# Sums of a seven-product output matmul moved from GpSimd to VectorE, with a planner that counts their shared port

## The chip, the cores and the metric

One Trainium2 chip, one of its cores. The time is device microseconds of one execution, the median of several. Engines: TensorE (PE) multiplies, VectorE (DVE), ScalarE (ACT) and GpSimd (POOL) work element by element, SyncE (SP) issues the DMAs, which start in the order of its queue.

## The reference

```python
# attention: batch 4, 12 heads, 448 tokens, 64 per head
scores = scale * np.matmul(q, k.transpose(0, 1, 3, 2))
scores = np.einsum('bhij,hg->bgij', scores, w_pre)
attn = exp(scores - max) / (sum + 1e-09)
attn = np.einsum('bhij,hg->bgij', attn, w_post)
x = np.matmul(attn, v)            # as [1792 tokens, 768]
# two products behind it
h = x @ w_in                      # [1792, 2048]
g = h * np.clip(h + 3.0, 0.0, 6.0) / 6.0
return g @ w_out                  # [1792, 768]
```

w_in and w_out are float64 and reach the kernel as 64-bit integers.

## The kernel before

The attention runs in 180 steps over rows of scores; a step has TensorE mix the heads, VectorE take the maximum (line 474), ScalarE the exponential (475), GpSimd the scaling and the low half of a two-part fp16 number (483, 486), and TensorE mix again (502). `av` (line 518) multiplies with v and leaves x, as a high and a low fp16 half (544, 545), in groups G0 to G7 (two for a batch). `moe1` (688) makes h and g of a group, 16 column blocks `fc` each, in three fp16 products (704), and stores g to DRAM (`gd`).

The last product, g @ w_out, is done with seven block products for a batch instead of eight: P1, P2 (stage 1) and P6, P7, P4, P5, P3 (stage 2). P1 and P2 take blocks of g and w_out as they are; the other five take sums and differences of blocks. Each operand is split into a high half (ScalarE, line 847) and a low half (VectorE, `scalar_tensor_tensor`, line 848), `ws_P` and `wg` or `gx_P` for short in the trace, and `product` (980) runs 24 matmuls for each of 3 row blocks m. `add` (1004) brings the PSUM sums together on VectorE.

w_out is decoded while the attention still runs: `w_out_decode` (678) is called every 4th step from step 72 on, with low urgency (priority 2000 and more), for 24 pieces of 128x512. It reads the integers, ScalarE and VectorE turn them into fp32 (585 to 600), and a store puts them into DRAM (`wod`, 683). After the attention, `w_one` loads 12 pieces for P1 and P2, and `w_two` loads all 24 again; `w_two_put` has GpSimd make four sums for each of six sets (`minus`, line 861) before the five splits. `g_two` (953) loads four blocks of g for each half of a batch and has GpSimd make four sums of 128x896 in the same way.

The order of all instructions on every engine is fixed when the kernel is built. A list planner (`Plan.run`, line 153) takes each operation's engine, a written duration, its inputs and outputs and a priority (lower goes first), and simulates: an engine that is free takes the ready operation of lowest priority. VectorE and GpSimd are independent of each other in it. The loads of the last product wait for `close_a` (line 802): all that the attention's buffers are used for must be done. The tiles of P6 and P7's w_out lie in a pool that opens when the last group of `moe1` no longer needs the first half of w_in (`close_w0`, 834), those of P4, P5 and P3 when `moe1` is through altogether (`close_w`, 830). The two buffers `slots` (863) hold the operands of P1 and P2; they follow the attention's `A` buffers in one ring of two.

Of the kernel before, what the change touches and what calls it, by code (L numbers as in the profile page):

```python
# [25 lines left out]
P = 128  # L26
# [18 lines left out]
G2_AT, G2_BY = 1080, 100  # L45
LATE_W = 'P4', 'P5', 'P3'
# [7 lines left out]
class Op:  # L54
    __slots__ = ("eng", "dur", "fn", "prio", "n", "succ", "order", "ready", "end", "bytes", "no", "mode", "takes", "then")
# [49 lines left out]
class Plan:  # L105
# [7 lines left out]
    STAY = 8.0  # L113

# [3 lines left out]
    def op(self, eng, dur, fn, r=(), w=(), prio=0.0, after=(), nbytes=0, mode=0):  # L118
        o = Op()
        o.eng, o.dur, o.fn, o.prio, o.bytes, o.mode = eng, dur, fn, prio, nbytes, mode  # L120
        o.succ, o.order, o.n, o.ready, o.no, o.end, o.takes, o.then = [], [], 0, 0.0, len(self.ops), None, [], None
        deps = {}

        def need(d):
            deps[d.no] = d

        for x in r:
            b, key = x if isinstance(x, tuple) else (x, None)
            for k, u, wr in b.uses:
                if wr and (k is None or key is None or k == key):  # L130
                    need(u)
        for x in w:
            b, key = x if isinstance(x, tuple) else (x, None)
            if b.pool and not b.uses and b not in o.takes:
                o.takes.append(b)
            if b not in self.bufs:
                self.bufs[b] = []
            self.bufs[b].append(o)
            for k, u, wr in b.uses:
                if k is None or key is None or k == key:  # L140
                    need(u)
        for u in after:
            need(u)
        for x, wr in [(x, False) for x in r] + [(x, True) for x in w]:
            b, key = x if isinstance(x, tuple) else (x, None)
            b.uses.append((key, o, wr))
        for d in deps.values():
            d.succ.append(o)
            o.n += 1
        self.ops.append(o)  # L150
        return o

    def run(self):
# [10 lines left out]
        bw, mode, then = 0.0, None, None  # L164

# [27 lines left out]
        while True:  # L193
# [34 lines left out]
            o.end = t + o.dur  # L228
            if e == "PE" and self.filler:
# [22 lines left out]
def body(ctx: ExitStack, tc: tile.TileContext, q4, kT, vj, wpre0, wpost0, ident0, w_in, w_out, outT):  # L252
# [32 lines left out]
    def dve(dur, fn, r, w, prio):  # L285
        return plan.op("DVE", dur, fn, r, w, prio)
# [295 lines left out]
    def decode(raw, o, n, st, prio, cost):  # L582
# [21 lines left out]
        return lambda: [dve(cost[2 + i], f, [raw] * (i > 0), [o], prio + 0.3 + 0.1 * i) for i, f in enumerate((b1, b2, b3))]  # L604

    def pow64(top, am1, t, p, r):
# [4 lines left out]
        DVE.tensor_scalar(r(), r(), 2.0 ** 14, None, op0=ALU.mult)  # L611

# [3 lines left out]
    def w_in_item(fc, after=()):  # L616
# [6 lines left out]
        o = buf(rot, [P, DM], F32, "wf", f"wf_i{fc}", 3)  # L623
        st, am1, t, r = (buf(rot, [P, 1], F32, f"wi_{x}", f"wi{x}_{fc}", 4) for x in ("st", "am", "t", "r"))
        dma(786432, lambda: SP.dma_start(raw(), w_in[fc]), [], [raw], at, after)
        rest = decode(raw, o, DM, (st, st), at, (0.81, 0.94, 0.5, 1.15, 1.25))
# [15 lines left out]
        if fc % 4 == 0:  # L642
            act(0.82, lambda: ACT.activation(h(), o(), AF.Copy, scale=r()), [o, r], [(w, (0, fc))], at + 2)
            dve(1.0, lambda: DVE.scalar_tensor_tensor(l(), o(), r(), h(), op0=ALU.mult, op1=ALU.subtract), [o, r, (w, (0, fc))], [(w, (1, fc))], at + 2)
# [25 lines left out]
    def w_out_read(k, raw, o, at, after):  # L670
        plan.op("SP", 0.5, lambda: SP.dma_start(raw()[:, :4 * P], w_out[k // 4, k % 4]), [], [raw], at, after, 524288)
        decode(raw, o, 4 * P, ((wo_st, k), lambda: wo_st()[:, k:k + 1]), at, (0.57, 0.66, 0.35, 0.64, 0.64))()
        if k == 11:
            w_out_scale(0, 12, 1, at + 2)
        if k == 23:
            w_out_scale(1, 24, 4, at + 2)

    def w_out_decode(k, at, after):
        d = wo_dram[k] = Buf(lambda: dram.tile([P, 4 * P], F32, name=f"wod_{k}"))
        raw = buf(rot, [P, NCC * P], I64, "stw", f"wo_{k}", 2)  # L680
        o = buf(rot, [P, DM], F32, "wf", f"wf_d{k}", 3)
        w_out_read(k, raw, o, at, after)
        dma(262144, lambda: SP.dma_start(d(), o()[:, :4 * P]), [o], [d], at + 5)
# [116 lines left out]
    for b, gi, at in scales:  # L800
        g_scale(b, gi, at + 8)
    close_a = plan.op("X", 0.0, ph_a.close, prio=0, after=[o for o in plan.ops])
# [12 lines left out]
    for z in (wpre0_f, wpost0_f, wpre8, wpost_n, wpost_h, wpost_l, T_all, *(z for k, g in rings.items() if k[0] == "T" for z in g.all)):  # L815
# [27 lines left out]
    def load(nbytes, fn, r, w, at, after):  # L843
        plan.op("SP", 0.5, fn, r, w, at, after, nbytes)

    def split(src, r, to, key, n, at, after, big):
        plan.op("ACT", 0.95 if big else 0.63, lambda: ACT.activation(to(0), src(), AF.Copy, scale=r()), [src.b, r], [key], at, after)
        dve(1.3 if big else 0.9, lambda: DVE.scalar_tensor_tensor(to(1), src(), r(), to(0), op0=ALU.mult, op1=ALU.subtract), [src.b, r], [key], at + 0.1)  # L848

    class View:  # L850
        def __init__(self, b, fn):
            self.b, self.fn = b, fn

        def __call__(self):
            return self.fn()

    def whole(b):
        return View(b, lambda: b())
# [4 lines left out]
    slots = [buf(apool, [P, 11520], F16, "A", f"wg_{i}", 2) for i in range(2)]  # L863

    def w_view(t, z, i):
        return t()[:, :6144].rearrange("p (z m f c) -> p z m f c", z=2, m=3, f=8)[:, z, i // 2, 4 * (i % 2):4 * (i % 2) + 4]

    def g_view(t, at, z):
        return t()[:, at:at + 1792].rearrange("p (z f n) -> p z f n", z=2, f=4)[:, z]

    WS = {}

    def w_item(i):
        m, q = divmod(i, 2)
        return 4 * m + q, 4 * m + q + 2, 12 + 4 * m + q, 14 + 4 * m + q

    def w_tile(name):
        return gbuf([P, 4 * P], F32, "wr", name, WR)

    def w_load(k, at, name):  # L880
        if k < WO_EARLY:
            t = w_tile(name)
            load(262144, lambda: SP.dma_start(t(), wo_dram[k]()), [wo_dram[k]], [t], at, [close_a])
        else:
            raw = gbuf([P, 4 * P], I64, "stw", f"{name}_raw", 2)
            t = w_tile(name)
            w_out_read(k, raw, t, at, [close_a])
        return t

    def w_put(name, t, i, at, z, after):  # L890
        src = View(t, lambda: t().rearrange("p (f c) -> p f c", f=4))
        b = WS[name]
        split(src, later_r(z), lambda y: w_view(b, y, i), (b, (name, i)), 4 * P, at, after, False)

    class LaterR:
        pass

    def later_r(z):
        return wo_r[z]

    def w_one(i, at):
        for name, k in zip(("P1", "P2"), w_item(i)[:2]):
            t = w_load(k, at, f"w{name}_{i}")
            w_put(name, t, i, at, 0, [close_a])

    def w_two(i, at):
        k11, k12, k21, k22 = w_item(i)
        a21, a22 = w_load(k21, at, f"w21_{i}"), w_load(k22, at + 1, f"w22_{i}")
        a11, a12 = w_load(k11, at + 2, f"w11_{i}"), w_load(k12, at + 3, f"w12_{i}")
        s1 = w_tile(f"ws1_{i}")  # L910
        todo2.append((i, at, a11, a12, a21, a22, s1))

    def w_two_put(i, at, a11, a12, a21, a22, s1):
        minus(s1, a21, a22, ALU.add, at, False, [close_a])
        minus(a21, a11, a21, ALU.subtract, at + 1, False)
        minus(a11, s1, a11, ALU.subtract, at + 2, False)
        minus(a12, a12, a11, ALU.subtract, at + 3, False)
        for j, (name, t) in enumerate((("P6", a11), ("P7", a21), ("P4", a22), ("P5", s1), ("P3", a12))):
            w_put(name, t, i, at + 4 + j, 1, [close_a, close_w if name in LATE_W else close_w0])

    GP, later_home = {}, []
# [4 lines left out]
    def g_load(b, kk, half, i, at):  # L926
        t = g_tile(f"g{kk}{half}_{b}_{i}_{at}")
        f = 8 * kk + 4 * i
        keys_ = [(g_dram[b], (k, gi)) for k in (f // 2, f // 2 + 1) for gi in range(1 + half)]
        load(458752, lambda: SP.dma_start(t(), g_dram[b]()[:, f:f + 4, half * NH:half * NH + NH]), keys_, [t], at, [close_a])  # L930
        return t

    def g_put(name, b, i, t, at, home):
# [8 lines left out]
        GP[name, b, i] = (lambda z: g_view(x, o, z)), (x, (name, b, i))  # L942
        split(whole(t), g_s[b], lambda z: g_view(x, o, z), (x, (name, b, i)), 4 * NH, at, after, True)

    def g_one(b, at):
        for kk, name in ((0, "P1"), (1, "P2")):
            for i in range(2):
                n = 4 * b + 2 * kk + i
                t = g_load(b, kk, 0, i, at + 10 * kk + i)
                home = (slots[n // 3], 6144 + 1792 * (n % 3)) if n < 6 else None  # L950
                g_put(name, b, i, t, at + 10 * kk + i + 2, home)
# [52 lines left out]
    def add(out, ps, u, us, key_o, key_u, after):  # L1004
        plan.op("DVE", 0.37, lambda: DVE.scalar_tensor_tensor(out(), ps()[:, :NH], us(), u(), op0=ALU.mult, op1=ALU.add), [ps, us, key_u], [key_o], -80, [after])

    def stage1(b, at):
        us = scale(0, b)
        ua = uas[b] = [lambda m=m: ua_all()[:, b, m * NH:(m + 1) * NH] for m in range(3)]
        for m in range(3):  # L1010
            ps = product("P1", b, m, at)
            act(0.35, lambda m=m, ps=ps: ACT.activation(ua[m](), ps()[:, :NH], AF.Copy, scale=us()), [ps, us], [(ua_all, (b, m))], -80)
# [25 lines left out]
    WS["P1"], WS["P2"] = slots  # L1038
    for b in range(B):
        g_one(b, -300 + 60 * b)  # L1040
        if b == 0:
            for i in range(6):
                w_one(i, -290 + i)
# [45 lines left out]
```

## Time and profile before

| | us |
|---|---|
| median of 3 runs | 847.67 |
| lowest, highest | 846.43, 854.39 |
| profiled execution | 839.76 |
| its span, first to last instruction | 837.9 |

The profile is of one execution. Its page gives the busy time of each engine and the chain of work that ended last; other views give a table of stretches, instructions in order of time, waits, and groups by line. A group of instructions is named as line, engine, operation, output <- inputs, and partitions x elements; `x24` is a count. The PE clock is the share of full speed that was granted.

### The profile page before, as it was taken

The numbers are of one execution on the slowest core, as the hardware profiler recorded it, in microseconds if no ns is written. First come the engines' busy times: TensorE is split into PE (matmuls) and PEld (weight loads), VectorE is DVE, ScalarE is ACT, GpSimd is POOL, SyncE is SP. The second block draws the span as 40 slices with busy tenths as digits, with TensorE's granted clock in tenths as the row PEclk, the third lists the DMA queues.
The fourth block names the chain that finished last, engine by engine and source line by source line (L and its number), as shares of the span: only waits on it lengthen the run. The fifth ranks groups of instructions, "written<-read, shape, count | busy, mean of one in ns | idle before, by whom it ended". The sixth has DMA issues, their size and how long they took to land.

```text
span 837.9 us, 27650 instructions
## 1 busy us (share of the span) xinstructions
PE 793.0 (95%) x11588; PEld 639.2 (76%) x11588; DVE 594.0 (71%) x1129; ACT 529.5 (63%) x1043; POOL 483.5 (58%) x590
## 2 busy tenths in 40 slices
PE   8997899999999999999999989999999957999998
PEld 2554567577777767677777767889999956999998
DVE  4588887788657656967775876753865999878432
ACT  2477879887986766868886778865844735233200
POOL 2245789878775635667574567764027588495300
PEclk9799999999999999999999999999999988999999
DMA  7979977886588678878879787632993651655101
GB/s 258 309 233 307 319 224 230 277 258 213 165 286 255 206 215 277 276 241 258 272 232 291 226 275 253 194 100 63 362 336 113 189 171 41 197 156 160 56 18 51
DMA packets 107649, 179.32 MB, mean 214 GB/s; under 512 B 8308, under 2 KB 80084, under 8 KB 107524
## 3 DMA queue, kind: packets, MB, share of 16 engines
q1 hardware_dynamic: 107524, 177.55, 67.8%
q8 instruction: 91, 1.49, 0.7%
q14 instruction: 34, 0.28, 0.1%
HBM read 112.33 MB, written 65.18 MB: 212 GB/s over the span
## 4 chain that ended last, share of the span: by engine, by line
PE 63%; DVE 11%; DMA 10%; POOL 6%; issue 4%; ACT 4%; SPq 1%; ACTq 0%; DVEq 0%; POOLq 0%
PE single L704 19%; PE single L988 18%; PE single L502 8%; PE single L467 6%; PE pair L376 6%; PE single L539 5%; DVE ws_P L848 3%; DMA wo<-in_w_out 3%; POOL el L486 2%; POOL e L483 2%; DMA wi<-in_w_in 2%; DVE nb L474 2%; DVE gx_P L848 1%; DMA v<-in_vj 1%; PE single L743 1%
## 5 line engine op out<-in xcount | busy, mean ns | idle before, releaser
L704 PE MATMUL single<-x,wi 128*128 128x208 f16 (+1 forms) x2304 | 228.9, 260 | 4.4 <-ACT e L475 2.9
L704 PEld LDWEIGHTS <-wi 128*128 128x128 f16 x2304 | 214.4, 98 | 23.5 <-issue 16.9
L486 POOL TENSOR_TENSOR el<-e,eh 128x448 f16<-128x448 f32 x156 | 168.3, 1098 | 48.2 <-ACT eh L485 46.3
L988 PEld LDWEIGHTS <-ws_P 128*128 128x128 f16 x1440 | 141.5, 100 | 17.4 <-DVE ws_P L848 7.7
L483 POOL TENSOR_SCALAR e<-e,r 128x448 f32<-128x448 f32 x180 | 128.2, 723 | 43.3 <-DVE r L478 39.0
L475 ACT ACTIVATE e<-single,nb 128x448 f32<-128x448 f32 x180 | 113.3, 637 | 33.6 <-DVE nb L474 32.8
L474 DVE TENSOR_REDUCE nb<-single 128x1 f32<-128x448 f32 x180 | 102.0, 614 | 21.6 <-PE single L467 21.3
L717 ACT ACTIVATE g<-single,three,uh 128x240 f32<-128x240 f32 (+1 forms) x128 | 68.9, 539 | 63.3 <-PE single L704 60.2
L719 DVE SCALAR_TENSOR_TENSOR g<-g,six,single 128x240 f32<-128x240 f32 (+1 forms) x128 | 56.3, 442 | 62.3 <-ACT g L717 60.3
L376 PE MATMUL pair<-ks,qx 64*64 64x448 f32 x736 | 92.3, 569 | 3.8 <-ACT s L408 3.7
L467 PE MATMUL single<-T_all,wpre 64*64 64x448 f32 (+1 forms) x720 | 90.0, 558 | 4.3 <-DMA T_all<-sd 2.5
L485 ACT ACTIVATE eh<-e 128x448 f16<-128x448 f32 x156 | 87.2, 578 | 7.9 <-POOL e L483 7.3
L988 PE MATMUL single<-gx_P,ws_P 128*128 128x224 f16 x720 | 76.1, 272 | 14.1 <-DVE gx_P L848 7.2
L408 ACT ACTIVATE s<-pair 120x896 f32<-120x896 f32 (+1 forms) x90 | 82.4, 916 | 9.0 <-PE pair L376 3.6
L502 PEld LDWEIGHTS <-eh 60*128 60x128 f16 x2496 | 66.8, 100 | 19.8 <-issue 17.1
L539 PEld LDWEIGHTS single<-A,v 128*64 128x64 f32 x1536 | 74.0, 137 | 9.9 <-ACT A L513 3.5
L539 PE MATMUL single<-A,v 128*64 128x120 f32 (+1 forms) x1536 | 77.7, 261 | 0.3 <-ACT e L475 0.3
L477 POOL TENSOR_SCALAR sm<-sm 128x2 f32<-128x2 f32 (+1 forms) x92 | 22.5, 245 | 93.2 <-ACT e L475 85.4
L502 PE MATMUL single<-wpost_h,eh 60*128 60x60 f16 x1248 | 72.5, 202 | 3.1 <-ACT e L475 1.7
L502 PE MATMUL single<-wpost_l,eh 60*128 60x60 f16 x1248 | 71.8, 202 | 2.0 <-issue 2.0
L502 PE MATMUL single<-wpost_h,el 60*128 60x60 f16 x1248 | 71.9, 202 | 0.3 <-POOL el L486 0.3
L988 PE MATMUL single<-wg,ws_P 128*128 128x224 f16 x720 | 69.3, 259 | 0.0
(250 smaller groups left out, 1231.6 us busy)
## 6 DMA issues: line engine op xcount, KB each, us to landing
T_all<-sd SPq DMA_DIRECT2D x88, 420.0 KB, 5.7
sd<-s SPq DMA_DIRECT2D x72, 420.0 KB, 5.4
wi<-in_w_in SPq DMA_DIRECT2D x16, 768.0 KB, 7.3
wo<-in_w_out SPq DMA_DIRECT2D x24, 512.0 KB, 6.4
gd<-g SPq DMA_DIRECT2D x32, 240.0 KB, 3.9
sd<-s SPq DMA_DIRECT2D x24, 315.0 KB, 5.1
gd<-g SPq DMA_DIRECT2D x32, 208.0 KB, 3.9
wod<-wf_d SPq DMA_DIRECT2D x24, 256.0 KB, 4.3
```

The lines of the kernel that those rows point to most:

```text
L376: PE.matmul(at[u]()[c:c + m], q()[r, pr, c:c + m], k()[r, pr % 3, :], start=True, stop=True)
L408: act(0.82, lambda: ACT.activation(st()[:n], ps()[:n, :, :S], AF.Copy), [ps], [st], at + 0.5)
L467: PE.matmul(ps[r]()[64 * u:64 * u + 64, :S], wpre8()[rows], T_all()[rows, slot, u], start=True, stop=True)
L474: dve(0.53, lambda r=r: DVE.tensor_reduce(nb()[:, r:r + 1], ps[r]()[:, :S], axis=AX.X, op=ALU.max, negate=True), [ps[r]], [(nb, r)], s + 0 ...
L475: act(0.62, lambda r=r: ACT.activation(e()[:, r], ps[r]()[:, :S], AF.Exp, bias=nb()[:, r:r + 1], accum_out=sm()[:, r:r + 1]), [ps[r], (nb, ...
L483: pool(0.63, lambda r=r: POOL.tensor_scalar(e()[:, r], e()[:, r], rr()[:, r:r + 1], 1.0, op0=ALU.mult, op1=ALU.mult), [rr], [(e, r)], s + ...
L485: act(0.47, lambda r=r: ACT.activation(eh()[:, r], e()[:, r], AF.Copy), [(e, r)], [(eh, r)], s + 0.65 + 0.3 * r)
L486: pool(1.02, lambda r=r: POOL.tensor_tensor(el()[:, r], e()[:, r], eh()[:, r], op=ALU.subtract), [(e, r), (eh, r)], [(el, r)], s + 0.7 + 0 ...
L502: PE.matmul(out, x()[rows, r, js], z()[rows], start=(i == 0), stop=(i == len(mix) - 1))
L539: PE.matmul(ps()[u * D:(u + 1) * D, k:k + n], v()[:, jc, g * D:(g + 1) * D], a()[:, jc * H + g, :n], start=(jc == 0), stop=(jc == NJ - 1))
L704: PE.matmul(pv(), wi_g[g]()[:, w, f0, cc, :], x()[:, z, cc, :n], start=(cc == 0 and i == 0), stop=(cc == 5 and i == 2))
L988: PE.matmul(ps()[:, :NH], w_view(w, y, 2 * m + i)[:, f], g(x)[:, f, :], start=(i == 0 and f == 0 and (y, x) == (0, 0)), stop=(i == 1 and f ...
```

## The change

- The sums of w_out's blocks are made where w_out is decoded, on VectorE (`w_sum`, `tensor_tensor`, 128x512): 24 of them. The pieces are decoded in another order, set by set, and all seven operands of a set are stored: 42 stores (P1, P2, P4 are pieces, P5, P6, P7, P3 sums) in place of 24. Behind the attention each operand is loaded as it is used, 42 loads of 256 KB in place of 36, all of P6's first, then P7's and so on. The scales of w_out come after all 24 pieces.
- The decoded tiles lie in one buffer `WF`, of three places for w_in and afterwards of four smaller ones for w_out.
- `minus`, the sums of g in `g_two`, goes from GpSimd to VectorE (32 of 128x896).
- `first_ones`: P1's six pieces of w_out and three of its eight blocks of g are loaded and split ahead of `close_a`, at priority 170 to 176, into `slots[0]` as soon as the attention leaves it. The blocks of g pass through the buffers of the raw integers.
- The planner has a port shared by VectorE and GpSimd: a marked operation of VectorE, and any of GpSimd, is made longer by 0.8 (VectorE) or 0.35 (GpSimd) of its overlap with the other's. Several written durations change.

```diff
+PRE_AT = 170
+    SHARE = {"DVE": 0.8, "POOL": 0.35}
...
+            if o.share:
+                other = port["POOL" if e == "DVE" else "DVE"]
+                o.end += self.SHARE[e] * max(0.0, min(o.dur, other - t))
+                port[e] = o.end
...
+    def w_place():
+        if not wr_ring.all:
+            z = Buf(None)
+            z.uses = [u for x in wf_ring.all[-3:] for u in x.uses]
+            wr_ring.all += [z] * 4
+        n = len(wr_ring.all)
+        return Buf(lambda: WF()[:, n % 4 * 4 * P:(n % 4 + 1) * 4 * P], wr_ring)
+
+    def w_store(name, i, t, at):
+        d = ws_dram[name, i] = Buf(lambda: dram.tile([P, 4 * P], F32, name=f"wsd_{name}_{i}"))
+        dma(262144, lambda: SP.dma_start(d(), t()), [t], [d], at)
+
+    def w_sum(out, x, y, op, at):
+        dve(0.69, lambda: DVE.tensor_tensor(out(), x(), y(), op=op), [x, y], [out], at, True)
+
+    def w_out_decode(n, at, after):
+        i, j = divmod(n, 4)
+        m, q = divmod(i, 2)
+        k = 4 * m + q + (12, 14, 0, 2)[j]
...
+        if j:
+            w_store((None, "P4", "P1", "P2")[j], i, o, at + 2)
+        if j == 1:
+            s1 = a_t["s"] = w_place()
+            w_sum(s1, a_t[0], o, ALU.add, at + 2)
+            w_store("P5", i, s1, at + 3)
+        elif j == 2:
+            w_sum(a_t[0], o, a_t[0], ALU.subtract, at + 2)
+            w_store("P7", i, a_t[0], at + 3)
+            w_sum(a_t["s"], a_t["s"], o, ALU.subtract, at + 2.1)
+            w_store("P6", i, a_t["s"], at + 3.1)
+        elif j == 3:
+            w_sum(o, o, a_t["s"], ALU.subtract, at + 2)
+            w_store("P3", i, o, at + 3)
+        if n == 23:
             w_out_scale(0, 12, 1, at + 2)
-        if k == 23:
             w_out_scale(1, 24, 4, at + 2)
-
-    def w_out_decode(k, at, after):
-        d = wo_dram[k] = Buf(lambda: dram.tile([P, 4 * P], F32, name=f"wod_{k}"))
...
-        dma(262144, lambda: SP.dma_start(d(), o()[:, :4 * P]), [o], [d], at + 5)
...
+    def minus(out, x, y, op, at, big, after=()):
+        plan.op("DVE", 1.15, lambda: DVE.tensor_tensor(out(), x(), y(), op=op), [x, y], [out], at, after, share=True)
...
+    def first_ones():
+        for i in range(6):
+            t, d = w_place(), ws_dram["P1", i]
+            load(262144, lambda t=t, d=d: SP.dma_start(t(), d()), [d], [t], PRE_AT + i, [])
+            w_split("P1", i, t, PRE_AT + i + 0.5, [])
+            if i % 2 == 0:
+                n = i // 2
+                b, j = divmod(n, 2)
+                raw = buf(rot, [P, NCC * P], I64, "stw", f"g1_{n}", 2)
+                v = View(raw, lambda raw=raw: raw()[:, :2 * NH].bitcast(F32).rearrange("p (f n) -> p f n", f=4))
+                src, keys_ = g_rows(b, 0, 0, j)
+                load(458752, lambda v=v, src=src: SP.dma_start(v(), src()), keys_, [raw], PRE_AT + i, [])
+                g_split("P1", b, j, v, slots[0], 6144 + 1792 * n, PRE_AT + i + 0.6, [])
...
-    def minus(out, x, y, op, at, big, after=()):
-        plan.op("POOL", 2.1 if big else 1.25, lambda: POOL.tensor_tensor(out(), x(), y(), op=op), [x, y], [out], at, after)
...
-    def w_two_put(i, at, a11, a12, a21, a22, s1):
-        minus(s1, a21, a22, ALU.add, at, False, [close_a])
-        minus(a21, a11, a21, ALU.subtract, at + 1, False)
-        minus(a11, s1, a11, ALU.subtract, at + 2, False)
-        minus(a12, a12, a11, ALU.subtract, at + 3, False)
...
+    for n, name in enumerate(("P6", "P7", "P4", "P5", "P3")):
+        for i in range(6):
+            w_item(name, i, 1000 + 50 * n + i)
```

## Rows read from the trace of the kernel before

**Rows 1.** The page: span, busy time by engine, chain by engine.

```profile
span 837.9 us, 27650 instructions
...
PE 793.0 (95%) x11588; PEld 639.2 (76%) x11588; DVE 594.0 (71%) x1129; ACT 529.5 (63%) x1043; POOL 483.5 (58%) x590
...
PE 63%; DVE 11%; DMA 10%; POOL 6%; issue 4%; ACT 4%; SPq 1%; ACTq 0%; DVEq 0%; POOLq 0%
```

**Rows 2.** Stretches: length, busy PE, PEld, DVE, ACT, POOL, then clock, DMA share, GB/s.

```profile
235.00:530.00 295.00, 285.84 (x5002) 218.93 (x4994) 211.31 (x447) 222.32 (x486) 180.31 (x240) 0.99 0.81 254
530.00:593.00 63.00, 63.00 (x1153) 53.13 (x1146) 34.09 (x72) 42.37 (x93) 33.36 (x50) 1.00 0.45 131
...
616.00:645.00 29.00, 29.00 (x323) 28.58 (x321) 16.74 (x32) 11.16 (x20) 18.47 (x13) 1.00 0.66 205
645.00:675.00 30.00, 30.00 (x316) 30.00 (x314) 26.36 (x24) 19.75 (x30) 16.36 (x9) 1.00 0.48 146
675.00:715.00 40.00, 25.87 (x202) 22.60 (x200) 39.83 (x33) 18.16 (x23) 31.25 (x16) 0.79 0.40 116
715.00:835.00 120.00, 119.67 (x1249) 119.42 (x1247) 71.25 (x96) 24.94 (x25) 48.96 (x20) 1.00 0.36 108
```

**Rows 3.** TensorE in order of time: start, length, what, idle time before.

```profile
564.76 5.14 PE L539 MATMUL single<-A,v 128*64 128x120 f32 x96
...
644.59 31.21 PE L988 MATMUL single<-gx_P,wg 128*128 128x224 f16 x324
675.63 1.50 PE L988 MATMUL single<-gx_P,ws_P 128*128 128x224 f16 x14
684.30 5.13 PE L988 MATMUL single<-gx_P,ws_P 128*128 128x224 f16 x35 [7.16 <-DVE gx_P L848]
...
711.04 20.14 PE L988 MATMUL single<-gx_P,ws_P 128*128 128x224 f16 x191 [2.22 <-DVE ws_P L848]
```

**Rows 4.** What TensorE waited for from 590 us on: total, times, longest.

```profile
PE single L988 <- DVE gx_P L848: 7.2, 1, 7.2
PE single L988 <- DVE ws_P L848: 7.0, 3, 3.4
```

**Rows 5.** Line 848, VectorE's low halves: ns minimum/median/maximum, first and last start.

```profile
L848 DVE SCALAR_TENSOR_TENSOR ws_P<-w,wo_r,ws_P x24: 735/1709/2571, 633.1 to 715.1; 128x512 f16<-128x512 f32 x24
L848 DVE SCALAR_TENSOR_TENSOR wg<-wP,wo_r,wg x12: 743/744/752, 591.6 to 612.6; 128x512 f16<-128x512 f32 x12
...
L848 DVE SCALAR_TENSOR_TENSOR gx_P<-t,gs,gx_P x4: 1135/1646/2964, 666.5 to 773.0; 128x896 f16<-128x896 f32 x4
```

**Rows 6.** Line 861, GpSimd's sums, in the same view.

```profile
L861 POOL TENSOR_TENSOR w<-w,w x12: 1264/1710/2121, 614.6 to 708.7; 128x512 f32<-128x512 f32 x12
```

**Rows 7.** Stretches with line 848 alone: busy VectorE and its count.

```profile
645.00:675.00 30.00, 24.27 (x18) 1.00 0.48 146
675.00:715.00 40.00, 37.19 (x24) 0.79 0.40 116
```

**Rows 8.** SP's queue in order of time: the first load behind `close_a`.

```profile
581.84 0.36 SPq L930 DMA_DIRECT2D g_-300_11092<-gd  x1
```

**Rows 9.** VectorE in order of time: the last piece of x.

```profile
616.10 0.48 DVE L545 SCALAR_TENSOR_TENSOR x<-single,vr,x 128x270 f16<-128x270 f32 x1
```

**Rows 10.** Groups by line: an addition of stage 2 (busy us, mean ns, idle before).

```profile
L1005 DVE SCALAR_TENSOR_TENSOR oP<-single,us,u 128x224 f32<-128x224 f32 x24 | 10.4, 444 | 19.9 <-PE single L988 19.9
```

**Rows 11.** The decoding of w_out (tile `wf_d`): ns minimum/median/maximum.

```profile
L596 DVE SCALAR_TENSOR_TENSOR wf_d<-wo,wf_d x24: 672/806/1416, 238.6 to 526.4; 128x512 int32<-128x512 int32 x24
L600 DVE SCALAR_TENSOR_TENSOR wf_d<-wo,wf_d x24: 669/748/1414, 239.5 to 527.7; 128x512 int32<-128x512 int32 x24
L683 SPq DMA_DIRECT2D wod<-wf_d x24: 325/343/551, 240.2 to 529.1; - x24
```

**Rows 12.** SP's waits at the stores of w_out: total, times, longest.

```profile
SPq L683 <- DVE wf_d L600: 17.0, 9, 5.3
SPq L683 <- DVE r L478: 13.8, 7, 3.2
```

More of the change, by code (lines that the diff above doesn't have):

```diff
@@ L54 @@
 class Op:
-    __slots__ = ("eng", "dur", "fn", "prio", "n", "succ", "order", "ready", "end", "bytes", "no", "mode", "takes", "then")
+    __slots__ = ("eng", "dur", "fn", "prio", "n", "succ", "order", "ready", "end", "bytes", "no", "mode", "takes", "then", "share")
 class Buf:
@@ L164, in run @@
         bw, mode, then = 0.0, None, None
+        port = {"DVE": 0.0, "POOL": 0.0}
         def push(o):
@@ L611, in pow64, with in_ring @@
         DVE.tensor_scalar(r(), r(), 2.0 ** 14, None, op0=ALU.mult)
+    WF, wf_ring, wr_ring = const([P, 3 * DM], F32, "WF", one), Ring(3), Ring(4)
+    def in_ring(ring, make):
+        return Buf(make, ring)
     wi_g = {}
@@ L801, in body, with load, split, __init__ @@
         g_scale(b, gi, at + 8)
+    def load(nbytes, fn, r, w, at, after):
+        plan.op("SP", 0.5, fn, r, w, at, after, nbytes)
+    def split(src, r, to, key, n, at, after, big):
+        plan.op("ACT", 0.95 if big else 0.63, lambda: ACT.activation(to(0), src(), AF.Copy, scale=r()), [src.b, r], [key], at, after)
+        dve(1.15 if big else 0.75, lambda: DVE.scalar_tensor_tensor(to(1), src(), r(), to(0), op0=ALU.mult, op1=ALU.subtract), [src.b, r], [key], at + 0.1, True)
+    class View:
+        def __init__(self, b, fn):
+            self.b, self.fn = b, fn
+        def __call__(self):
+            return self.fn()
@@ new lines, in whole, with w_view, g_view @@
+    def whole(b):
+        return View(b, lambda: b())
+    def minus(out, x, y, op, at, big, after=()):
+        plan.op("DVE", 1.15, lambda: DVE.tensor_tensor(out(), x(), y(), op=op), [x, y], [out], at, after, share=True)
+    WS, GP = {}, {}
+    slots = [buf(apool, [P, 11520], F16, "A", f"wg_{i}", 2) for i in range(2)]
+    def w_view(t, z, i):
+        return t()[:, :6144].rearrange("p (z m f c) -> p z m f c", z=2, m=3, f=8)[:, z, i // 2, 4 * (i % 2):4 * (i % 2) + 4]
+    def g_view(t, at, z):
+        return t()[:, at:at + 1792].rearrange("p (z f n) -> p z f n", z=2, f=4)[:, z]
@@ new lines, in body, with w_split, g_split, g_rows @@
+    WS["P1"] = slots[0]
+    def w_split(name, i, t, at, after):
+        b = WS[name]
+        split(View(t, lambda: t().rearrange("p (f c) -> p f c", f=4)), wo_r[int(name not in ("P1", "P2"))], lambda y: w_view(b, y, i), (b, (name, i)), 4 * P, at, after, False)
+    def g_split(name, b, i, t, x, o, at, after):
+        GP[name, b, i] = (lambda z: g_view(x, o, z)), (x, (name, b, i))
+        split(t, g_s[b], lambda z: g_view(x, o, z), (x, (name, b, i)), 4 * NH, at, after, True)
+    def g_rows(b, kk, half, i):
+        f = 8 * kk + 4 * i
+        return (lambda: g_dram[b]()[:, f:f + 4, half * NH:half * NH + NH]), [(g_dram[b], (k, gi)) for k in (f // 2, f // 2 + 1) for gi in range(1 + half)]
@@ L814, in body @@
     users = {id(u[1]): u[1] for (pid, tag), g in rings.items() if pid in (id(one), id(rot), id(dsc)) for z in g.all for u in z.uses}
-    for z in (wpre0_f, wpost0_f, wpre8, wpost_n, wpost_h, wpost_l, T_all, *(z for k, g in rings.items() if k[0] == "T" for z in g.all)):
+    for z in (wpre0_f, wpost0_f, wpre8, wpost_n, wpost_h, wpost_l, T_all, *wf_ring.all, *wr_ring.all[4:], *(z for k, g in rings.items() if k[0] == "T" for z in g.all)):
         users.update({id(u[1]): u[1] for u in z.uses})
@@ L890, in w_put @@
[L890 to L911, printed above, removed]
@@ L923, in g_tile @@
+    later_home = []
     def g_tile(name):
@@ L927, in g_load @@
         t = g_tile(f"g{kk}{half}_{b}_{i}_{at}")
-        f = 8 * kk + 4 * i
-        keys_ = [(g_dram[b], (k, gi)) for k in (f // 2, f // 2 + 1) for gi in range(1 + half)]
-        load(458752, lambda: SP.dma_start(t(), g_dram[b]()[:, f:f + 4, half * NH:half * NH + NH]), keys_, [t], at, [close_a])
+        src, keys_ = g_rows(b, kk, half, i)
+        load(458752, lambda: SP.dma_start(t(), src()), keys_, [t], at, [close_a])
         return t
@@ L941, in g_put @@
         x, o = home
-        GP[name, b, i] = (lambda z: g_view(x, o, z)), (x, (name, b, i))
-        split(whole(t), g_s[b], lambda z: g_view(x, o, z), (x, (name, b, i)), 4 * NH, at, after, True)
+        g_split(name, b, i, whole(t), x, o, at, after)
     def g_one(b, at):
@@ L1004, in add @@
     def add(out, ps, u, us, key_o, key_u, after):
-        plan.op("DVE", 0.37, lambda: DVE.scalar_tensor_tensor(out(), ps()[:, :NH], us(), u(), op0=ALU.mult, op1=ALU.add), [ps, us, key_u], [key_o], -80, [after])
+        plan.op("DVE", 0.44, lambda: DVE.scalar_tensor_tensor(out(), ps()[:, :NH], us(), u(), op0=ALU.mult, op1=ALU.add), [ps, us, key_u], [key_o], -80, [after])
     def stage1(b, at):
@@ L1036, in stage2 @@
                     add(ua[m], ps, ua[m], us, ka, ka, close_w)
-    WS["P1"], WS["P2"] = slots
+    WS["P2"] = slots[1]
     for b in range(B):
```

78 lines of the change are left out of this document (22 added, 56 removed).

## The prediction

> **What bounds the kernel now.** I read the page first, then a table by stage, then TensorE's order of time in the one stage that stands out, and last the lines that run there. [rows 1] gives the span of 837.9 us: TensorE is busy in 95% of it, the other three engines in 58 to 71%. So only a stretch in which TensorE starves can be worth much. [rows 2] finds it. From 616 to 675 us TensorE is busy without a break, from 715 to 835 too (119.67 of 120), but from 675 to 715 it is busy for only 25.87 of 40, at a mean granted clock of 0.79 (1.00 stands for 2.4 GHz, 0.50 for the lower level of 1.2 GHz, which comes with the idle time), while VectorE is busy for 39.83 of the 40. This is where the output product passes from stage 1 (P1, P2) to stage 2 (P6, P7, P4, P5, P3).
>
> [rows 3] shows it in order of time: 324 matmuls of stage 1 in one piece, 14 of stage 2, then nothing until 684.30, and no unbroken work before 711.04. [rows 4] names who was late: VectorE, with the low halves of the split operands (`gx_P`, `ws_P`, line 848), for 7.2 and 7.0 us.
>
> What is it worth? At full speed one matmul takes 119.67 / 1249 = 0.0958 us [rows 2]. The 40 us have room for 418; 202 ran. The loss is 216 x 0.0958 = 20.7 us, idle time and low clock together.
>
> Why was VectorE late? [rows 5] compares one instruction with itself. The split of a `w_out` piece (128x512) takes 0.744 us in stage 1, hardly varying, while GpSimd does nothing; in stage 2 its median is 1.709 and its maximum 2.571. The split of 128x896 takes 1.135 at its quickest and 2.964 at its slowest. GpSimd makes the sums (line 861) at the same time, and its 128x512 sum goes from 1.264 to 2.121 as well [rows 6]. The excess of a disturbed split, up to 2.571 - 0.735 = 1.84 us, is about one such GpSimd instruction. The Trainium skill, SBUF — State Buffer, section Who interferes with whom, says that a VectorE instruction with two SBUF inputs and a GpSimd instruction that reads SBUF exclude each other for their whole length; this trace agrees, by the 1.84 us.
>
> **The change part by part, near the end.** *GpSimd's sums leave stage 2.* 24 sums of `w_out` go to the decoding, 32 sums of g go to VectorE. From 645 to 715 us VectorE ran 18 + 24 = 42 splits in 24.27 + 37.19 = 61.5 us [rows 7]. By size they are 28 of 128x512 and 14 of 128x896; undisturbed they cost 28 x 0.744 + 14 x 1.135 = 36.7 us. Gain on VectorE: 24.7 us. Against it: of the sums of g, 12 fall before 715 us (8 of batch 0, 4 of batch 1). The trace has no 128x896 sum on VectorE. Below, nothing is possible only if they run where VectorE idles (12.3 us of 29 between 616 and 645, [rows 2]); above, the worst disturbed split, 2.964. GpSimd has nothing left to disturb them, so I take the undisturbed split of the same size, 1.135: 12 x 1.135 = 13.6 us. Net 24.7 - 13.6 = 11.1 us.
>
> *The first block early.* 6 splits of P1 and 3 of g (6 x 0.744 + 3 x 1.135 = 7.9 us of VectorE) and their loads move ahead of the end of the attention, at 530 to 593 us, where VectorE is busy for 34.09 of 63 us and ScalarE for 42.37 [rows 2]. Their cover is that idle time; they wait for `slots[0]`, a buffer that the last but one product of the attention frees at 569.90 us [rows 3], so ScalarE (nine halves of about 0.7 to 1 us) may push the closing of the phase, and with it the first load at 581.84 [rows 8], by 2 us or so; behind a half that waits on ScalarE stand the last exponentials, and TensorE's matmuls behind those. TensorE itself gains nothing there: it is 63.00 of 63 busy. But the work on VectorE that follows starts 7.9 us sooner, also because the last piece of x, whose low half waited behind these splits until 616.10 [rows 9], lets the first product's last group, and the pools that its end opens for `ws_P`, come sooner.
>
> Together VectorE is 11.1 + 7.9 = 19.0 us ahead at the place where 20.7 us were lost. I count 19.0 us of gain and leave 1.7 us as what stays. The 42 loads in place of 36 don't add there: 6 of the 42, with 3 of g, are moved ahead, 36 pieces remain, and the DMA share between 645 and 715 is 0.40 to 0.48 [rows 2].
>
> *Does VectorE last through stage 2?* Per batch it has 10 splits and 8 sums of 1.135 [rows 5] and 18 additions of 0.444 [rows 10]: 28.4 us, against 360 x 0.0958 = 34.5 us of TensorE. It does, at 82%.
>
> **The change part by part, in the attention.** 24 sums of 128x512 go in between 235 and 530 us. The nearest rows are the decoding's own two-input instructions of that size [rows 11]: minimum 0.67, medians 0.75 and 0.81, maximum 1.42. I take 0.8: 19 us more on VectorE, which is idle for 295 - 211.31 = 83.7 us there [rows 2]. Bounds of what reaches the end: nothing, since the sums have the lowest urgency of all; or the whole 19 us, if each holds up a softmax step by its length. TensorE is idle for 9.2 us there beside 211 busy us of VectorE, 0.044 us per us, so 19 us bring about 1. The 18 more stores go through SP's queue: it waited at the present 24 for 17.0 + 13.8 = 30.8 us in 16 waits [rows 12], 1.9 each, with the loads of the next scores (line 459) behind it. I add 1 us for them, 2 us in all; below, no loss; above, see the rivals. That the planner counts the shared port and puts other durations on the decoding changes the order of the instructions a little everywhere before 530 us; I can price that at no more than the idle 9.2 us of TensorE either way, and take nothing.
>
> **Sum.** The profiled execution took 839.76 us; 839.76 - 19.0 + 2 = 822.8. The runs shown have a median of 847.67, 0.94% above it. Carried over by that ratio: 830.5 us.
>
> **Rivals.** *(A) VectorE is still late* at the start of stage 2: the pools for `ws_P` open no sooner, the sums of g stand in front of the splits in its order, and only the net 11.1 us less about 2 are gained. For it: VectorE is 97% full from 645 to 715. Against it: 12.3 us idle just before. 839.76 - 9 = 831, as a median 838.5: faster by 1.1%, on the edge.
>
> *(B) The sums pay their full price in the attention.* GpSimd is busy for 180.31 of 295 us there [rows 2], with sums of its own that read two operands. If each new sum waits for one GpSimd instruction of 1.264 us [rows 6] and holds it up in turn, it is 24 x (0.8 + 1.264) = 50 us on VectorE, more than half of which the idle time takes: 15 to 20 us of the gain are given back, and the median is 846 to 850. The rule of the Trainium skill cited above, taken by itself, speaks for this one and against the change. Against it: the 48 decoding instructions with two inputs already run under the same GpSimd work with medians near the minimum [rows 11].
>
> *(C) Slower: SP's queue.* 18 more stores in order, each waiting 1.9 us for its sum and 0.34 us to issue [rows 11], make 18 x 2.24 = 40 us in which the loads of scores stand behind. If over 27 us of that reach TensorE, the gain is gone and 1% more: about 856 us. For it: DMA holds 10% of the chain that ended last [rows 1]. Against it: SP's waits at the present stores, 30.8 us, left TensorE idle for 9.2 us in all.
>
> *(D) The change doesn't do what it says*: another wait (loads, a buffer ring of 8 for the sums of g) takes the place of VectorE's, and stage 2 starts as raggedly as now: 842 to 853.
>
> **How the numbers follow.** Chances: forecast 0.62, A 0.14, B 0.11, C 0.08, D 0.05. One per cent (8.5 us) is about what a measurement of this kernel can tell from no change. Faster by more: the forecast and two thirds of A, 0.71; within 1%: the rest of A, most of B and D, 0.18; slower: C, and a part of B and D, 0.11. The likeliest time is 830.5. The range's lower end takes the whole 20.7 us, no cost in the attention, and half of the distance between the profiled time and the median: 816. Its upper end takes A with 5 us lost in the attention: 844. What lies above it is B, C and D in part, under 0.2.
>
> **What would show it.** Right: in the profile after, TensorE busy in all of the 40 us after stage 1 with a granted clock of 1.0; the splits of 128x512 at 0.74 us in stage 2; no GpSimd work there but single columns; VectorE's sums of 128x896 near 1.1 us; 235 to 530 us lengthened by no more than 3 us. Wrong: idle time before the first `ws_P` matmuls still put down to VectorE (A); sums above 1.4 us and longer GpSimd instructions in the attention (B); longer waits of SP at the stores and TensorE waiting for `T_all` (C); stage 2 waiting for loads (D).

## The result and the profile after

| | before | after |
|---|---|---|
| median of the first four runs of each, us | 848.79 (846.43 to 854.39) | 822.58 (814.10 to 825.42) |
| profiled execution, us | 839.76 | 821.90 |
| its span, us | 837.9 | 820.0 |

The ratio is 0.9665, with an interval of 0.9579 to 0.9752. The changed kernel was timed twice more on other chips, further down: 0.9770 (0.9691 to 0.9848) and 0.9746 (0.9678 to 0.9813). So it is faster by 2.3 to 3.4% by the medians, and by 1.5 to 4.2% with the intervals. The forecast was 830.5 us, 816 to 844.

First the page of the kernel after, with the busy times of [rows 1]:

```profile
span 820.0 us, 27643 instructions
...
PE 786.2 (96%) x11581; PEld 637.2 (78%) x11581; DVE 596.6 (73%) x1185; ACT 527.1 (64%) x1043; POOL 372.9 (45%) x534
...
PE 71%; DMA 11%; ACT 6%; DVE 4%; POOL 3%; issue 2%; SPq 1%; ACTq 0%; DVEq 0%; POOLq 0%
```

VectorE is busy for as long as before (596.6 against 594.0 us) and yet its share of the chain that ended last falls from 11% to 4%: it does as much work, but less of it where TensorE waits for it. GpSimd is busy for 110.6 us less.

Then the table of stretches, as in [rows 2] (length; busy PE, PEld, DVE, ACT, POOL; granted clock, DMA share, GB/s):

```profile
235.00:530.00 295.00, 286.12 (x5124) 216.54 (x5124) 226.14 (x462) 226.60 (x496) 192.49 (x247) 0.99 0.85 269
530.00:593.00 63.00, 62.48 (x994) 54.81 (x988) 40.77 (x86) 41.17 (x89) 30.38 (x45) 1.00 0.46 137
...
645.00:675.00 30.00, 30.00 (x319) 30.00 (x317) 24.06 (x35) 23.19 (x36) 0.00 (x0) 1.00 0.80 249
675.00:715.00 40.00, 40.00 (x420) 40.00 (x418) 35.99 (x50) 13.89 (x15) 0.00 (x0) 1.00 0.49 147
```

From 675 to 715 us TensorE is now busy for all of the 40 us, at a granted clock of 1.00 (2.4 GHz) in place of 0.79, and 420 matmuls run there where 202 did. And TensorE in order of time (start, length, what), to be laid beside [rows 3]:

```profile
648.62 1.31 PE L1014 MATMUL single<-wg 128*128 128x224 f16 x12
649.77 28.91 PE L1014 MATMUL single<-gx_P,wg 128*128 128x224 f16 x300
678.52 34.66 PE L1014 MATMUL single<-gx_P,ws_P 128*128 128x224 f16 x360
713.02 34.66 PE L1014 MATMUL single<-wg,ws_P 128*128 128x224 f16 x360
747.52 34.66 PE L1014 MATMUL single<-gx_P,ws_P 128*128 128x224 f16 x360
782.02 34.66 PE L1014 MATMUL single<-wg,ws_P 128*128 128x224 f16 x360
```

Each batch of stage 2 is one unbroken piece of 360 matmuls. From 648.62 to the end of the last, 816.68, 1752 matmuls take 168.1 us, 0.0959 each: nothing is lost any more. Before, 1764 matmuls from 644.59 [rows 3] to 834.67 took 190.1 us, 20.9 more than 1764 x 0.0959.

Below I use this measure for every kernel: *the loss in stage 2* is the time from the last unbroken stretch of stage 1 to the last matmul, less 0.0959 us for each matmul in it. And *the start* is the time at which that stretch begins, moved back by 0.0959 us for each matmul that is missing to 1764. Before: start 644.6, loss 20.9. After: start 648.62 - 12 x 0.0959 = 647.5, loss 0. The span falls by 17.9: 20.9 won in stage 2, 2.9 given back ahead of it, 0.1 left over (the 2.9 compare one execution with one; more on this at the end).

### The profile page after: what moved, and what is told of

It is laid out like the page before. It is cut to its first block, busy times and chain, and to the rows that moved or that the text cites. A ratio compares the mean times of both kernels' runs of the same rounds, so it can differ in the third digit from the quotient of the medians.

```text
span 820.0 us, 27643 instructions
## 1 busy us (share of the span) xinstructions
PE 786.2 (96%) x11581; PEld 637.2 (78%) x11581; DVE 596.6 (73%) x1185; ACT 527.1 (64%) x1043; POOL 372.9 (45%) x534
## 4 chain that ended last, share of the span: by engine, by line
PE 71%; DMA 11%; ACT 6%; DVE 4%; POOL 3%; issue 2%; SPq 1%; ACTq 0%; DVEq 0%; POOLq 0%
PE single L1014 24%; PE single L745 21%; PE single L547 8%; PE single L510 7%; PE pair L384 6%; PE single L475 5%; DMA sd<-s 4%; DMA T_all<-sd 4%; DMA wo<-in_w_out 2%; ACT e L483 2%; ACT s L416 2%; POOL el L494 1%; POOL e L491 1%; ACT eh L493 1%; DMA wi<-in_w_in 1%
## 5 line engine op out<-in xcount | busy, mean ns | idle before, releaser
L494 POOL TENSOR_TENSOR el<-e,eh 128x448 f16<-128x448 f32 x156 | 170.4, 1110 | 39.0 <-ACT eh L493 35.9
L491 POOL TENSOR_SCALAR e<-e,r 128x448 f32<-128x448 f32 x180 | 130.6, 736 | 42.5 <-DVE r L486 37.9
L1014 PEld LDWEIGHTS <-ws_P 128*128 128x128 f16 x1440 | 138.0, 98 | 0.0
L475 PE MATMUL single<-T_all,wpre 64*64 64x448 f32 (+1 forms) x720 | 86.5, 557 | 5.3 <-DMA T_all<-sd 4.0
L547 PEld LDWEIGHTS single<-A,v 128*64 128x64 f32 x1536 | 75.7, 139 | 11.5 <-ACT eh L493 4.0
L485 POOL TENSOR_SCALAR sm<-sm 128x2 f32<-128x2 f32 (+1 forms) x92 | 26.1, 284 | 97.7 <-ACT e L483 91.0
L1014 PE MATMUL single<-gx_P,ws_P 128*128 128x224 f16 x720 | 69.3, 259 | 0.0
```

The costliest lines, as they stand in the source:

```text
L475: PE.matmul(ps[r]()[64 * u:64 * u + 64, :S], wpre8()[rows], T_all()[rows, slot, u], start=True, stop=True)
L491: pool(0.63, lambda r=r: POOL.tensor_scalar(e()[:, r], e()[:, r], rr()[:, r:r + 1], 1.0, op0=ALU.mult, op1=ALU.mult), [rr], [(e, r)], s + ...
L494: pool(1.02, lambda r=r: POOL.tensor_tensor(el()[:, r], e()[:, r], eh()[:, r], op=ALU.subtract), [(e, r), (eh, r)], [(el, r)], s + 0.7 + 0 ...
L547: PE.matmul(ps()[u * D:(u + 1) * D, k:k + n], v()[:, jc, g * D:(g + 1) * D], a()[:, jc * H + g, :n], start=(jc == 0), stop=(jc == NJ - 1))
L1014: PE.matmul(ps()[:, :NH], w_view(w, y, 2 * m + i)[:, f], g(x)[:, f, :], start=(i == 0 and f == 0 and (y, x) == (0, 0)), stop=(i == 1 and f ...
```

## Experiments: which part of the change fills the gap

**The kernel after, and the kernel after with one part undone.** Four kernels on one chip, where the kernel before had a median of 845.31 us.

> The changed kernel itself, so that the next ones are compared on the same chip. All theories: 0.967 of the kernel before, about 822 us, TensorE busy without a break from stage 1 to the end.

Measured: 824.88 us, 0.9770 (0.9691 to 0.9848). Start 650.5, loss 0.

The sums of g back on GpSimd:

```diff
-        plan.op("DVE", 1.15, lambda: DVE.tensor_tensor(out(), x(), y(), op=op), [x, y], [out], at, after, share=True)
+        plan.op("POOL", 2.1, lambda: POOL.tensor_tensor(out(), x(), y(), op=op), [x, y], [out], at, after)
```

> The changed kernel with the sums of g back on GpSimd (the planner still counts the port). If the shared port was what made VectorE late: 32 of the 56 sums, two thirds of their time, run beside the splits again, splits of 128x896 reach 2 to 3 us, and 8 to 12 us of the gain go: 831 to 835 us. If the order of the work and the first block made early were the cause: no change, 820 to 825 us.

Measured: 822.0 us, 0.9729 (0.9650 to 0.9807). The 831 to 835 us that I gave to the port didn't come: nothing is lost by the edit. The port shows all the same. The low halves of that kernel (line 848; ns minimum/median/maximum), then its table of stretches:

```profile
L848 DVE SCALAR_TENSOR_TENSOR ws_P<-wP,wo_r,ws_P x30: 735/743/2579, 636.8 to 687.4; 128x512 f16<-128x512 f32 x30
...
L848 DVE SCALAR_TENSOR_TENSOR gx_P<-t,gs,gx_P x4: 1140/2604/2900, 670.7 to 754.6; 128x896 f16<-128x896 f32 x4
```

```profile
645.00:675.00 30.00, 30.00 (x319) 30.00 (x317) 25.73 (x29) 21.61 (x34) 9.50 (x4) 1.00 0.68 213
675.00:715.00 40.00, 40.00 (x420) 40.00 (x418) 37.86 (x44) 15.87 (x17) 25.90 (x10) 1.00 0.60 181
```

Some splits of 128x896 still take 2.6 to 2.9 us beside GpSimd, and VectorE is busy for 37.86 of 40 us, but TensorE runs without a break. In this kernel, splits slowed by the port do no harm.

The first block made behind the attention:

```diff
-    first_ones()
...
-                if kk == 0 and n < 3:
-                    continue
...
+                w_item("P1", i, -290 + i)
                 w_item("P2", i, -289.5 + i)
```

> The changed kernel without the first block made early: P1's pieces of w_out and of g are loaded and split behind the end of the attention, as before. If VectorE's lead is the sum of parts as I had it (11.1 us from the sums, 7.9 us from the first block), 8 us of lead are gone and most of them show: 826 to 831 us, with TensorE waiting for VectorE early in stage 2. If the sums alone bring it: 821 to 824 us. If the first block brings it: 838 us or more.

Measured: 824.15 us, 0.9777 (0.9710 to 0.9844), 0.7 us below the kernel after on the same chip. TensorE's only wait behind 590 us is for VectorE's first splits, at the very start of stage 1:

```profile
PE single L1011 <- DVE wg L848: 1.1, 2, 0.7
```

Leaving the first block out costs 1.1 us there and nothing in stage 2. The 7.9 us of lead that I gave it buy nothing.

The planner without the shared port:

```diff
-    SHARE = {"DVE": 0.8, "POOL": 0.35}
+    SHARE = {"DVE": 0.0, "POOL": 0.0}
```

> The changed kernel with the planner's shared port taken out (both shares 0), all else the same. If the planner matters little: 819 to 826 us, a difference in the order of the attention alone. If it is the better order that brings the gain: above 832 us.

Measured: 827.05 us, 0.9812 (0.9745 to 0.9878), 2.2 us above the kernel after, with intervals that overlap. The loss in stage 2 is 0 as well; what differs is the start, 655.8 in the profiled execution, which was the slowest of the four (830.21).

So none of these three is needed for the gap to close. What they have in common is the part that was left in all of them: w_out's 24 sums are gone from stage 2, and its operands are loaded as finished pieces. The new written durations and the buffer `WF` were left in them too; no run undoes these.

**That part alone.** The three edits above together, which leaves the sums of w_out in the decoding, the stores, the loads product by product, and the written durations. This and the next three runs are on another chip, where the kernel before had a median of 844.34 us; the kernel after wasn't run there.

> Only one part of the change: the sums of w_out made while it is decoded, and stored. The sums of g are on GpSimd, the first block is made behind the attention, both shares are 0. If this part alone frees VectorE (24 sums beside the splits gone, no chain of loads and sums in front of a split): 822 to 830 us, TensorE without a break in stage 2. If two parts are needed (each of the others could be spared singly): 833 to 842 us, with a break near the start of stage 2.

Measured: 829.09 us, 0.9811 (0.9747 to 0.9875). TensorE in order of time around the start of stage 2:

```profile
653.87 28.91 PE L1011 MATMUL single<-gx_P,wg 128*128 128x224 f16 x300
682.62 1.50 PE L1011 MATMUL single<-gx_P,ws_P 128*128 128x224 f16 x14
684.38 26.42 PE L1011 MATMUL single<-gx_P,ws_P 128*128 128x224 f16 x274 [0.26 <-DVE gx_P L848]
711.33 7.06 PE L1011 MATMUL single<-gx_P,ws_P 128*128 128x224 f16 x72 [0.53 <-DVE oP L1028]
718.22 34.66 PE L1011 MATMUL single<-wg,ws_P 128*128 128x224 f16 x360
```

The same joint as in [rows 3], with waits of 0.26 and 0.53 us where there were 7.16 and 2.22. The loss is 1.1 us of the 20.9. So this part closes all but 5% of the gap by itself. The medians stand 4 to 6 us above those of the kernel after on the other two chips; in the profiled executions 1.1 us of the distance is this loss, and 1 to 4 us the start (651.6 against 647.5 to 650.5).

The same kernel with other priorities of the stored operands, which were meant to have them taken set by set, as before, and not all of P6's first:

```diff
-            w_item(name, i, 1000 + 50 * n + i)
+            w_item(name, i, 1004 + 50 * i + n)
```

> As the run with the sums of w_out alone, but the stored operands are loaded and split set by set, as the kernel before does, not all of P6's first. If fewer sums beside the splits are the cause: within 4 us of that run. If the order (P6's six pieces first) is: 8 us or more above it, TensorE waiting for the low halves of w_out.

Measured: 828.06 us, 0.9806 (0.9739 to 0.9873), 1.0 us below, with a loss of 0.7 us. But the edit doesn't bring back the order of the kernel before. The loaded operands go through a ring of eight buffers, and it is filled in the order in which the program names the operands: all of P6's, then P7's, and so on. A load waits until the piece eight places ahead of it is split, whatever its priority. The traces show it. Until the last product of `moe1` is through, only P6 and P7 have a place for their halves, twelve pieces in all. In the kernel before, two low halves of w_out (line 848, tile `ws_P`) run ahead of that point (645); in this run, where it lies at 658, all twelve do (length, busy VectorE and its count, then as in [rows 7]):

```profile
620.00:645.00 25.00, 4.55 (x2) 1.00 0.59 184
```

```profile
635.00:658.00 23.00, 8.68 (x12) 1.00 0.69 203
```

So the order of the operands stays an open rival. The part that closes the gap takes the sums out of stage 2 and lets the six pieces of a product come one behind the other, which the sums in place, made set by set, don't; no run has the one without the other.

**The sums left in stage 2, but on VectorE.** Is it the port, then? In the kernel before all 56 sums go to VectorE in place:

```diff
-        plan.op("POOL", 2.1 if big else 1.25, lambda: POOL.tensor_tensor(out(), x(), y(), op=op), [x, y], [out], at, after)
+        plan.op("DVE", 1.15 if big else 0.75, lambda: DVE.tensor_tensor(out(), x(), y(), op=op), [x, y], [out], at, after)
```

> The kernel before with all 56 sums of stage 2 on VectorE where they stand; GpSimd does nothing there. By my sums VectorE gets 24.7 us back and 12 x 1.1 + 24 x 0.69 = 30 us on top before 715 us: as late as before, 0.995 to 1.01 of the kernel before. If the splits slowed by GpSimd are the whole cause: 0.975 to 0.985.

Measured: 838.57 us, 0.9922 (0.9880 to 0.9964), between my two expectations. GpSimd is idle in stage 2 and every split undisturbed, but most of the gap stays. The low halves of w_out, to be laid beside [rows 5]; then TensorE in order of time, and what ScalarE waited for from 645 to 745 us:

```profile
L848 DVE SCALAR_TENSOR_TENSOR ws_P<-w,wo_r,ws_P x24: 740/744/751, 646.8 to 724.4; 128x512 f16<-128x512 f32 x24
```

```profile
658.32 31.21 PE L988 MATMUL single<-gx_P,wg 128*128 128x224 f16 x324
689.37 7.06 PE L988 MATMUL single<-gx_P,ws_P 128*128 128x224 f16 x72
699.59 0.53 PE L988 MATMUL single<-gx_P,ws_P 128*128 128x224 f16 x2 [3.16 <-ACT gx_P L847]
701.52 18.17 PE L988 MATMUL single<-gx_P,ws_P 128*128 128x224 f16 x166 [1.40 <-DVE gx_P L848]
```

```profile
ACT ws_P L847 <- DVE ws L861: 10.4, 3, 5.3
...
ACT wg L847 <- DVE g_3000.1_12540 L861: 6.5, 1, 6.5
ACT ws_P L847 <- DVE w L861: 6.1, 11, 0.9
```

Start 658.3, last matmul 841.39: 183.1 us for 1764 matmuls, a loss of 13.9. Freeing the port, net of the sums that VectorE then makes itself, is worth 20.9 - 13.9 = 7.0 us by these two executions (the medians stand 5.8 us apart); I had expected about nothing. What is new is the wait of ScalarE's high half for a sum that stands in VectorE's queue behind other splits, and TensorE waits for both engines in turn.

And with the sums of g alone on VectorE (the 24 of w_out stay on GpSimd):

```diff
-        plan.op("POOL", 2.1 if big else 1.25, lambda: POOL.tensor_tensor(out(), x(), y(), op=op), [x, y], [out], at, after)
+        plan.op("DVE" if big else "POOL", 1.15 if big else 1.25, lambda: (DVE if big else POOL).tensor_tensor(out(), x(), y(), op=op), [x, y], [out], at, after)
```

> The kernel before with the sums of g alone on VectorE; the 24 sums of w_out stay on GpSimd in stage 2. By my sums: half of the 24.7 us back, 13.6 us on top: no gain, 0.99 to 1.005 of the kernel before. If the sums of g were the ones that slow the splits: 0.98 or less.

Measured: 836.29 us, 0.9904 (0.9857 to 0.9951), at the edge of the first expectation (0.99). Start 650.6, last matmul 829.71: a loss of 9.9 us, so it halves the gap, where I had expected none of it to close. Against this run, the one above, with w_out's 24 sums on VectorE as well, loses 4.0 us more. With 32 of its 56 sums gone GpSimd meets fewer of the low halves of w_out (line 848; the median was 1709 in [rows 5]):

```profile
L848 DVE SCALAR_TENSOR_TENSOR ws_P<-w,wo_r,ws_P x24: 734/741/1756, 639.1 to 713.2; 128x512 f16<-128x512 f32 x24
```

## Experiments: what the sums cost in the attention

Four kernels on one chip, the kernel before at 845.12 us. In the first two the plan's durations are unchanged, so every engine has the order of the kernel after.

```diff
+        n = 4 * P if op is ALU.add else 1
-        dve(0.69, lambda: DVE.tensor_tensor(out(), x(), y(), op=op), [x, y], [out], at, True)
+        dve(0.69, lambda: DVE.tensor_tensor(out()[:, :n], x()[:, :n], y()[:, :n], op=op), [x, y], [out], at, True)
```

> The changed kernel, its order of instructions unchanged, with 18 of the 24 sums in the decoding cut to one column (the six P5 sums are whole): part of the computation is left out. 12 us less on VectorE in the attention. If the sums hide there: 0 to 2 us less. If each holds up a step (the rival of the full price): 8 to 12 us less.

Measured: 823.92 us, 0.9752 (0.9695 to 0.9808).

```diff
+    scr = const([P, 4 * P], F32, "scr", one)
-        dve(0.69, lambda: DVE.tensor_tensor(out(), x(), y(), op=op), [x, y], [out], at, True)
+        dve(0.69, lambda: (DVE.tensor_tensor(scr(), x(), y(), op=op), DVE.tensor_tensor(out(), x(), y(), op=op)), [x, y], [out], at, True)
```

> The changed kernel, its order unchanged, with each of the 24 sums in the decoding made twice (the first time into a spare tile). 17 to 20 us more on VectorE in the attention, which the plan doesn't know of. If VectorE's idle time there takes it: 0 to 4 us more. If each holds up a step: 15 to 20 us more.

Measured: 826.1 us, 0.9777 (0.9720 to 0.9833).

> The changed kernel on the same chip as the three runs with shortened, doubled and fewer transfers, to be compared with them: 0.967 to 0.98 of the kernel before.

Measured: 823.23 us, 0.9746 (0.9678 to 0.9813). The sums in the three kernels, from their groups by line (shortened, doubled in two rows, as they are; busy us, mean ns, idle time before):

```profile
L699 DVE TENSOR_TENSOR WF<-WF 128x1 f32<-128x1 f32 (+1 forms) x24 | 9.6, 407 | 2.4 <-DMA wsd_P<-WF 2.3
```

```profile
L699 DVE TENSOR_TENSOR scr<-WF 128x512 f32<-128x512 f32 x24 | 20.2, 843 | 0.1
L699 DVE TENSOR_TENSOR WF<-WF 128x512 f32<-128x512 f32 x24 | 19.9, 829 | 0.6
```

```profile
L698 DVE TENSOR_TENSOR WF<-WF 128x512 f32<-128x512 f32 x24 | 20.4, 855 | 3.8 <-DMA wsd_P<-WF 3.6
```

Between 9.6 and 40.1 us of sums, 30.5 us of VectorE, the medians differ by 2.2 us, inside the intervals, which is 0.07 us per us. Each holding up a step by its length would have made it 30. So the sums hide for the most part in VectorE's idle time. How well is known only roughly: the four executions of each kernel spread over 7 to 8 us, and a difference of up to 8 us can't be excluded.

Fewer stores:

```diff
+        if name in ("P5", "P6", "P3"):
+            ws_dram[name, i] = ws_dram["P4", i]
+            return
```

> The changed kernel with 24 stores of w_out in place of 42: P5, P6 and P3 aren't stored, and P4's piece is loaded in their place, so part of the computation is left out; all instructions of the other engines are there. If SP's queue costs little: within 3 us of the changed kernel. If the 18 stores hold up the loads of scores (the rival): 5 us or more below it.

Measured: 832.08 us, 0.9870 (0.9823 to 0.9916): 8.9 us *slower* than the kernel after, with 4.7 MB less to store. Neither expectation held. The stores aren't what costs time. But without them the planner puts the instructions in another order: in the traces, about a quarter of VectorE's stand in another sequence than in the kernel after, where two executions of one program agree but for a few. That the order is what costs the time is argued, not shown. Its stretch at the end of the attention, and below it that of the kernel after on the same chip:

```profile
530.00:593.00 63.00, 58.10 (x995) 47.84 (x993) 42.73 (x89) 39.91 (x85) 29.39 (x43) 0.98 0.54 167
```

```profile
530.00:593.00 63.00, 62.48 (x1053) 54.97 (x1046) 41.47 (x88) 42.16 (x90) 31.35 (x48) 1.00 0.46 142
```

TensorE is idle for 4.9 of the 63 us; its longest single wait there is 2.8 us, put down to an exponential. The start is 658.7 against 649.2, and stage 2 has no loss. Which of the displaced instructions is at fault was not followed further.

## Why the prediction was right, point by point

**The place and its worth: right.** TensorE's starvation at the start of stage 2 was the bound, VectorE was the late engine, and 20.7 us were to be had there (20.9 by the whole stage). All of it came; I had left 1.7 us as rest. (VectorE was 95% full from 645 to 715, 26.36 + 39.83 of 70 us, not 97%.)

**What fills it: right in the total, wrong in the parts.** I added 11.1 us (the port, net of g's sums on VectorE) and 7.9 us (the first block) to 19.0. The runs show that the second is worth nothing in stage 2, that g's sums may stay on GpSimd, and that the part with w_out's 24 sums in the decoding brings 19.8 of the 20.9 us alone. So it is luck that the two terms add up to nearly what came. (Of the 42 splits that I counted, one runs across 675 us and stands in both stretches; with 41 the first term is about 0.7 us larger.) The failed step is the one that counts VectorE's busy time as the whole of its lateness. It took the disturbed durations of the splits and made everything else additive. What it left out is what stands in front of the splits of a set: four loads, four sums on one engine (four of the five splits take one), a high half on ScalarE, and only then the low half. It also left out that the sets come one behind the other: the last low half of w_out starts at 715.1, 39.5 us behind the first matmul of stage 2 [rows 3, rows 5]. With the sums stored as finished operands a split waits for one load, and the last starts 6.5 us behind (685.0 and 678.52, the row below). That the sums in place on an undisturbed VectorE still leave a loss of 13.9 us, with the last low half 35.0 us behind (724.4 and 689.37), shows that taking GpSimd away isn't enough. How that rest divides between VectorE's time for the sums, the length of the chain and the order of the operands was not separated: both runs that keep sums of w_out in stage 2 have all three. I had also expected the first block to let the end of `moe1` come sooner. It doesn't show: the start is 648.3 without the block, and 647.5 to 650.5 with it.

**VectorE lasts through stage 2: right.** Its sums of 128x896 take 1.08 us (I took 1.135), its splits of 128x512 0.747 as stated, and it is busy for 35.99 of the 40 us, 90%, with TensorE full. My 82% was for a batch without w_out's splits. These rows answer [rows 5] and [rows 6]:

```profile
L848 DVE SCALAR_TENSOR_TENSOR ws_P<-wP,wo_r,ws_P x30: 742/747/753, 637.2 to 685.0; 128x512 f16<-128x512 f32 x30
...
L861 DVE TENSOR_TENSOR t<-g,g_1080.1_11535 x1: 1077/1077/1077, 631.2 to 631.2; 128x896 f32<-128x896 f32 x1
```

**The sums in the attention: right.** 24 sums took 20.2 us in the kernel after (I took 19), the median one 0.694 and the longest 1.419, like the decoding's instructions of [rows 11]. The 2 us that I added for sums and stores stand beside 2.2 us, with the wide margin said above, between 9.6 and 40.1 us of sums. Rival B, the full price of 15 to 20 us, is refuted here: the longest of the sums is 1.419 - 0.669 = 0.75 us above the shortest.

**The stores: right that they cost little, wrong about what surrounds them.** SP waited at the 42 stores for 42.4 us in 34 waits. Before, it was 42.4 us as well, in 23: to the two rows of [rows 12] comes a third that I had left out, 11.4 us in 6 waits for `g` (line 719), and 0.2 us more. So rival C falls. But I priced the new order of the attention at nothing. The run with fewer stores came out 8.9 us longer, most likely by its order, and the one without the shares starts 5 to 8 us later in its profiled execution (its median is 2.2 us longer). An order can so cost more than any term that the sum has in the attention. That it was small in the kernel after is luck.

**The size: the term that was off is the carrying over to the median.** On the profile's own scale I had 822.8 us, a gain of 17.0, and the profiled execution took 821.90, a gain of 17.9. The medians fell by more: by 26.2 us in the first runs, by 20.4 and 21.9 on the other chips. I had assumed that the profiled execution of the new kernel would stand as far below its median as that of the old one, 0.94%. It stands 0.1% below it (821.90 and 822.58); the old one's was one of its faster executions, 839.76 among 835 to 855 us (one at 985 aside). Set against the medians of 844 to 845 us on the other chips, the 20.9 us of stage 2 alone give about 824, which is what was measured there (823.2 and 824.9). So the 2.9 us that the pair of profiles shows as given back in the attention are probably the luck of one execution; that is argued, since no second profile of the kernel before was taken. The lower end of my range also doesn't come out of its own terms: 839.76 - 20.7 is 819.1, and with half of the distance to the median, 4 us, it is 823, not 816. The first median, 822.58, lies just below that, the other two just above.

## What to carry to other kernels

Where an engine is late at one joint, count not only its busy time there but the chain that stands in front of each of its instructions; here a sum made and stored in an earlier phase took both out, and moving it to another engine in place took out only a part. Undo each part of a change singly and also try the likely one alone: three of four parts could be spared here, and the total had hidden it. And see in the trace that an edit does what it is meant to: a priority that a buffer ring overrules changes little. One profiled execution may stand 1% off its median, as much as a measurement tells from no change: the loss at a joint is a firmer number than the distance of two spans.

## What was not expected of the hardware

A split slowed by GpSimd to 2.6 to 2.9 us, more than twice its 1.14, cost nothing with VectorE busy for 37.86 of 40 us. How far the operands are ahead seems to decide, not the slowed instruction. And the last stretch of stage 1 starts at 647.5, 650.5 and 649.2 us in three profiled executions of the kernel after, while the 168 us behind it repeat to 0.1: the spread between these executions arises ahead of it.
